# Where the second matrix of an MLP begins, and where weight sums, a late normalization and the last output product stand

## The chip, the cores and the metric

The kernel runs on one core of a Trainium2 chip. The metric is the device time of one execution in microseconds. Five engines work side by side, each on its own instruction list in order: TensorE (PE; its weight loads are PEld), VectorE (DVE), ScalarE (ACT), GpSimd (POOL) and SyncE (SP), which here issues nearly all DMAs. They wait for one another through semaphores.

## The reference

A transformer block on 2048 rows of 512: modulated layernorm, an attention in four segments of 512 rows with 32 heads of 16 and a memory M, z carried from segment to segment, an output projection, a second modulated layernorm, and an MLP of 1792 with gelu.

```python
h = _layernorm(x) * (1 + ca) + sa
for s in range(4):                       # inside _A_ref
    p = softmax(qs @ ks.T * scale + mask)
    a_mem = (phi(qs) @ M) / (phi(qs) @ z + 1e-6)
    o = g * a_mem + (1 - g) * (p @ vs)
    M, z = M + phi(ks).T @ vs, z + phi(ks).sum
x = x + ga * (o @ wo)
h = _layernorm(x) * (1 + cb) + sb
x = x + gb * (gelu(h @ w1 + b1) @ w2 + b2)
```

All matrices are fp32; the kernel splits most operands into a high and a low part (fp32r) and forms each product of 128 x 128 by 128 x 512 as three matmuls: high-high, low-high and high-low.

## The kernel before

The order of every engine's list is written out by hand (`manual_schedule`): instructions enter their engine's list in the order in which the Python code calls them.

First come the projections of the four segments (to about 190 us). Then the attention runs over 64 pairs of heads P; a "stack" Q is two pairs, a unit U is two stacks, four units make a segment. In each P the `order` strings of PRM place score parts for the row maxima of pair P + 4 (S), the exponentials of pair P (T), and slots c0 to c9. Work of other kinds has a position, ten times P plus the slot: `pv` (probabilities times values), `m_rows` and `m_put` (negative maxima, put into qst by a small DMA on ACT's queue), `load_stacks`, `pv_out` (stores TD), `pv_in`, `am_in`, `den`, `rb_in`, `mem_mix`, `mix`, `o_hi`, `o_lo` (the late normalization of a unit: the row sums dn go to memory as RD and come back spread out as rbB; memory term amB times rm; then the sum, and its split oh, ol). `ln` holds the positions at which the rows of segments 0 and 1 are loaded (`ln2_load`, tile xt), get statistics, `ln2_rstd` (crs, on POOL) and `ln2_apply`; `ht` those of the transposes `ln2_turn` of segment 0. `load_w1` fetches weight tiles wa for units 0 and 1 of the MLP at P = 58 and 60.

What is left over when the loop ends is called by `rest(U, names)` in the junction (L1102 to L1154): output products `wo_seg(s, b, gs)` of segments 2 and 3 (g counts the four units of a segment, b the four row blocks), their results `wo_out`, the transposes of segment 1, and the preparation of the MLP.

The MLP works in two passes p, each over two segments. Its first matrix w1 is multiplied by a scheme with seven products in place of eight for each pair of f blocks (a "quad" n; 7 quads a pass): b11, b21, t2, t1, t3, t4, b22 (`prod`). Their right sides are differences of the transposed rows (`r_sub`, split by `r_hi`, `r_lo`), their left sides the weights wa and the sums wb (`w_sub`, on POOL; split by `w_hi`, `w_lo`). X (bx), Y (by) and V (bv) are banks, two of each. t4 adds onto t3 in X, once ACT has copied t3 out (s3); b22 adds onto t2 in V. In `quad(n)` the two last products t4 and b22 of unit n - 1 stand between the products of unit n; an eighth call per pass does these alone (`last`). `g_out` does the gelu and stores a block to GD. `bg(n, i, ...)` hangs background work on step i of quad n.

The second matrix (`ffn2`) takes 28 steps m a pass, one g block each: twelve matmuls into four banks (`accs`). `load_g` brings g back from GD into a ring of four tiles, `split_g` splits it on ACT and DVE into a ring of three pairs. In pass 0 the w2 blocks are loaded in pairs (`load_w2`), scaled, and split on the way.

The tag wm has four buffers that wa, wb and w2r share in turn; amB had one.

Of the kernel before, what the change touches and what calls it, by code (L numbers as in the profile page):

```python
# [55 lines left out]
 'ht': [465, 474, 481, 494],  # L56
 'ln': [[312, 339, 374, 408], [560, 597, 612, 624]],
# [31 lines left out]
 'w1at': [58, 60],  # L89
 'mpre': 'a',  # L90
# [12 lines left out]
def block_kernel(ctx: ExitStack, tc: tile.TileContext, x, wq, wk, wv, wo, betaq, betam,  # L103
# [482 lines left out]
    with ExitStack() as pb:  # L586
# [255 lines left out]
        wa = {}  # L842
        NP = 64
# [122 lines left out]
    with ExitStack() as pc:  # L966
# [33 lines left out]
        wb = {}  # L1000

        def w_sub(j, i):
            if i == 0:
                wb[j] = wmp.tile([128, 4, 2, 128], F32, tag="wm", bufs=4, name=f"wb{j}")
            a, b = wa[j], wb[j]
            x, y = ((a[:, 2], a[:, 3]), (b[:, 0], a[:, 0]), (a[:, 0], a[:, 2]), (a[:, 1], b[:, 1]))[i]
            pool.tensor_tensor(out=b[:, i], in0=x, in1=y, op=ALU.add if i == 0 else ALU.subtract)  # L1007

# [37 lines left out]
        TAIL = 100  # L1046
# [4 lines left out]
        def quad(n, first, last):  # L1051
            def step(i):
                for f, a in bgs.pop((TAIL + n if last else n, i), ()):
                    f(*a)

            X, Y, V_, t2 = bx[n % 2], by[n % 2], bv[n % 2], s2[n % 2]
            X_, V__, t2_ = bx[(n - 1) % 2], bv[(n - 1) % 2], s2[(n - 1) % 2]
            if not last:
                prod(n, "b11", X, True)
                act.activation(s1, X, AF.Copy)  # L1060
            if not first:
                add(s3, V__)
                g_out(n - 1, s3, s3, 1, 1)
            step(0)
            if not last:
                prod(n, "b21", Y, True)
                add(s1, Y)
            step(1)
            if not first:
                prod(n - 1, "t4", X_, False)  # L1070
            if not last:
                g_out(n, s1, s1, 0, 0)
            if not first:
                g_out(n - 1, X_, s4, 1, 0)
            step(2)
            if not last:
                prod(n, "t2", X, False)
                act.activation(t2, X, AF.Copy)
            step(3)
            if not first:  # L1080
                prod(n - 1, "b22", V__, False)
                add(t2_, V__)
            step(4)
            if not last:
                prod(n, "t1", V_, True)
            if not first:
                g_out(n - 1, t2_, t2_, 0, 1)
            step(5)
            if not last:
                prod(n, "t3", X, False)  # L1090
                act.activation(s3, X, AF.Copy)
            step(6)
# [48 lines left out]
        r_hi(0, "t2")  # L1141
        for i in range(2, 4):
            w_lo(0, i)
# [96 lines left out]
        bg(6, 3, load_w2, 6)  # L1240
# [5 lines left out]
        ring = [[s1, s2[1 - p], s3, s4] for p in range(2)]  # L1246

        def load_g(p, m):
            sp.dma_start(ring[p][m % 4], GD[2 * p + m // FB][m % FB])

        def split_g(p, m):
            h, l = gx[0](f"gh{p}{m}"), gx[0](f"gl{p}{m}")
            ghs.append((h, l))
            split(h, l, ring[p][m % 4], v, act)
# [14 lines left out]

        for f in range(4, FB, 2):  # L1270
            if f + 4 < FB:
                fbg(0, f - 4, load_w2, f + 4)
            fbg(0, f - 4, scale_w2, f)
            fbg(0, f - 4, hi_w2, f)
            fbg(0, f - 3, lo_w2, f)
# [112 lines left out]
```

## Time and profile before

| | us |
|---|---|
| three timed runs | 819.32, 819.83, 821.99 (median 819.83) |
| the profiled execution | 820.48 |
| its span | 818.8 |
| PE busy | 788.6 |
| DVE, ACT, POOL busy | 555.7, 467.8, 333.9 |
| end of the projections, first scores | about 190 |
| last value product, first output product of segment 2 | 483.0 |
| first product of the MLP (b11 of quad 0) | 505.3 |
| first w2 product of pass 0, of pass 1 | 588.1, 736.5 |

A timeline row gives start, duration, engine, line, operation, output <- inputs with their shapes, how many were merged, and in brackets how long the engine stood idle before it and what released it. SPq and ACTq rows are the moments at which a DMA is issued, not its transfer. A window row gives for each engine the busy time in that stretch and the number of instructions, then the mean granted TensorE clock (1.00 is full), the share of the DMA engines in use and what they moved.

### The profile page before, as it was taken

Reading aid. Unit: us, or ns where it says so; the run is one execution under the profiler, and the core shown is the slowest. Engines: PE = TensorE matmul, PEld = TensorE weight load, DVE = VectorE, ACT = ScalarE, POOL = GpSimd, SP = SyncE. Lnnn points to the kernel's source line nnn. Section 1 sums busy time; section 2 is a strip of 40 time slices with the busy share of each in tenths; the row PEclk is TensorE's granted clock in tenths of the full one; section 3 lists DMA queues with packets and bytes.
Section 4 is the critical chain, followed back from the end, with each engine's and each line's share of the span. In section 5 each row is a group of like instructions: output and inputs, shape, how many; then the busy total and the mean of one; then the engine's idle time right before and its main releaser. Section 6 shows DMA issues by size and latency. Waiting matters only on the chain.

```text
span 818.8 us, 14152 instructions
## 1 busy us (share of the span) xinstructions
PE 788.6 (96%) x4585; PEld 535.2 (65%) x4585; DVE 555.7 (68%) x1405; ACT 467.8 (57%) x914; POOL 333.9 (41%) x558
## 2 busy tenths in 40 slices
PE   8999999999999999999999798999899999989998
PEld 4877777865444355445544246878688888868887
DVE  6685696569888877886688648875569765522423
ACT  3565645565787766776687574677553336652221
POOL 1347375542487645687766562342000313300000
PEclk9999999999999999999999899999999999999999
DMA  9597756594655675775667634755656624435443
GB/s 338 181 309 257 268 187 206 166 353 131 169 175 159 188 206 179 228 211 156 193 174 217 199 124 144 245 178 176 231 172 200 198 91 155 167 131 154 151 143 116
DMA packets 107522, 156.10 MB, mean 191 GB/s; under 512 B 16180, under 2 KB 55476, under 8 KB 107064
## 3 DMA queue, kind: packets, MB, share of 16 engines
q1 hardware_dynamic: 104952, 153.23, 58.4%
q10 hardware_dynamic: 2496, 1.97, 0.8%
q8 instruction: 36, 0.59, 0.3%
q14 instruction: 38, 0.31, 0.1%
HBM read 93.95 MB, written 60.83 MB: 189 GB/s over the span
## 4 chain that ended last, share of the span: by engine, by line
PE 75%; DVE 7%; ACT 6%; DMA 6%; issue 3%; POOL 3%; ACTq 0%; SPq 0%; DVEq 0%; POOLq 0%
PE bx L1032 8%; PE pv L737 7%; PE att L697 6%; PE att L608 6%; PE bx L1309 5%; PE q L314 5%; PE by L1309 5%; PE bv L1309 5%; PE bv L1032 4%; PE k L314 4%; PE v L465 3%; PE spare L1309 2%; PE mm L814 2%; PE mm L1309 2%; PE by L1032 2%
## 5 line engine op out<-in xcount | busy, mean ns | idle before, releaser
L615 DVE CUSTOM_DVE_ANT_0 dump<-att,maskb 128x512 bf16<-128x512 f32 (+2 forms) x384 | 192.4, 553 | 27.4 <-PE att L608 24.5
L712 ACT ACTIVATE pt<-att 128x512 f32<-128x512 f32 (+1 forms) x256 | 126.2, 560 | 45.3 <-PE att L697 44.9
L700 POOL TENSOR_SCALAR_AFFINE_SELECT pt<-pt 128x256 f32<-128x256 f32 x256 | 101.4, 413 | 82.8 <-ACT pt L712 49.0
L697 PE MATMUL att<-qst,kst 99*128 99x512 bf16 (+3 forms) x512 | 109.1, 304 | 7.2 <-ACT pt L723 3.0
L608 PE MATMUL att<-kst,qst 96*128 96x512 bf16 (+2 forms) x384 | 95.1, 330 | 2.8 <-DMA qst<-QD 2.4
L1007 POOL TENSOR_TENSOR wb<-wa 128x256 f32<-128x256 f32 x28 | 26.9, 962 | 155.5 <-DMA wa<-in_w 147.4
L737 PE MATMUL pv<-pt,V 128*32 128x512 f32 (+2 forms) x992 | 89.0, 450 | 0.0
L137 DVE TENSOR_TENSOR gl<-s,gh 128x512 fp32r<-128x512 f32 x56 | 39.9, 712 | 69.5 <-ACT gh L134 69.4
L697 PEld LDWEIGHTS <-kst 99*128 99x128 bf16 x512 | 43.5, 98 | 61.8 <-issue 43.0
L134 ACT ACTIVATE gh<-s 128x512 fp32r<-128x512 f32 x56 | 35.1, 630 | 83.2 <-PE spare L1309 38.9
L723 ACT ACTIVATE pt<-att 128x512 f32<-128x512 f32 (+1 forms) x128 | 56.9, 509 | 21.9 <-PE att L608 19.9
L608 PEld LDWEIGHTS <-qst 96*128 96x128 bf16 x384 | 33.4, 98 | 42.7 <-issue 25.2
L737 PEld LDWEIGHTS pv<-pt,V 128*32 128x32 f32 x992 | 22.3, 109 | 36.8 <-issue 27.1
L1041 DVE TENSOR_TENSOR s<-bv,s 128x512 f32<-128x512 f32 x28 | 19.3, 688 | 37.7 <-PE bv L1032 29.2
L619 DVE TENSOR_REDUCE nm<-att 128x2 f32<-128x256 f32 x64 | 27.2, 426 | 23.5 <-PE att L655 19.2
L1037 ACT ACTIVATE s<-s,b1t 128x512 f32<-128x512 f32 x42 | 30.3, 721 | 16.2 <-DVE s L1041 16.1
L615 DVE DVE_READ_ACCUMULATOR2_ANT nm<- 128x1 f32 x384 | 31.9, 83 | 0.0
L1309 PE MATMUL bx<-w2h,gh 128*128 128x512 f32 (+1 forms) x70 | 26.4, 377 | 4.1 <-ACT gh L134 4.1
L510 POOL TENSOR_TENSOR q<-qr,q 128x512 bf16<-128x512 f32 x16 | 18.7, 1167 | 27.9 <-ACT q L509 27.7
L501 POOL TENSOR_SCALAR qp<-qp 128x512 f32<-128x512 f32 x12 | 18.8, 1564 | 23.1 <-ACT qp L496 23.1
L1309 PE MATMUL bx<-w2h,gl 128*128 128x512 f32 (+1 forms) x70 | 26.4, 377 | 0.2 <-DVE gl L137 0.2
L314 PE MATMUL q<-Ahl,wqh 128*128 128x512 f32 x64 | 25.9, 404 | 0.5 <-DVE Ahl L137 0.5
(324 smaller groups left out, 2049.4 us busy)
## 6 DMA issues: line engine op xcount, KB each, us to landing
GD<-s SPq DMA_DIRECT2D x56, 256.0 KB
s<-GD SPq DMA_DIRECT2D x56, 256.0 KB
kst<-KD SPq DMA_DIRECT2D x32, 384.0 KB
qst<-QD SPq DMA_DIRECT2D x32, 384.0 KB
TD<-ts SPq DMA_DIRECT2D x32, 256.0 KB
wa<-in_w SPq DMA_DIRECT2D x28, 256.0 KB
QD<-q SPq DMA_DIRECT2D x16, 384.0 KB
KD<-k SPq DMA_DIRECT2D x16, 384.0 KB
```

The costliest lines, as they stand in the source:

```text
L134: act.activation(hi, src, AF.Copy)
L137: lo_eng.tensor_tensor(out=lo, in0=src, in1=hi.bitcast(F32), op=ALU.subtract)
L314: pe.matmul(ps, a[:, k, 128 * g:128 * g + 128], b[k], start=(k == 0 and i == 0), stop=(k == KB - 1 and i == 2))
L608: pe.matmul(ps, q_of(P, h, i), k_of(P, h, 128 * (i + 1)), start=True, stop=True)
L615: v.tensor_tensor_reduce(out=dump[n_dump[0] % 2][:, :n], in0=src, in1=maskb[:, 512 - n:], scale=-1.0, scalar=-4 * NEG, op0=ALU.add, op1=AL ...
L697: pe.matmul(ps, k[:99, e, 128 * j:128 * j + 128], q[:99, e, 128 * j:512], start=True, stop=True)
L700: pool.affine_select(out=t, in_=t, pattern=pattern, compare_op=ALU.is_ge, fill=0.0, base=0, channel_multiplier=-1)
L712: act.activation(pt[:, h, :], ps[:, :n], AF.Exp, scale=0.25)
L723: act.activation(pt, pv_, AF.Exp, scale=0.25)
L737: pe.matmul(ps[32 * c:32 * c + 32, lo:hi], V[4 * s + j][:, VW * hd:VW * hd + 32], pt[:, c % 2, lo - o:hi - o], start=start, stop=stop)
L1032: pe.matmul(ps, a[:, i, k, :], b[k], start=start and k == 0 and c == 0, stop=k == 1 and c == 2, skip_group_check=not start)
L1309: pe.matmul(ps, a[:, c], w[:, lo:hi], start=(f == 0 and i == 0), stop=(last and i == 2))
```

## The change

The positions of segment 0's transposes and of segment 1's layernorm are other ones; amB gets two buffers; `w_sub` is defined earlier, and for units 0 and 1 it runs on DVE at positions 642 and 650. In the junction the late normalization of unit 15, the splits and the third and fourth part (g = 2, 3) of segment 3's output products stand in other places; `close_wo` no longer has products and hangs on step 2 of quad 0. The eighth quad call is gone: after the seventh, the w2 steps begin, and t4 and b22 of the last unit follow steps 0 and 1 (`tail`). The first two g blocks of a pass get a tile of the tag wm (gr), loaded at step 1 of the last quad; the loads of w2 blocks 6 to 12 stand at steps 0, 1, 2 and 4 of the second matrix.

```diff
- 'ht': [465, 474, 481, 494],
- 'ln': [[312, 339, 374, 408], [560, 597, 612, 624]],
+ 'ht': [481, 501, 521, 541],
+ 'ln': [[312, 339, 374, 408], [590, 618, 630, 636]],
+ 'wsub': [642, 650],
-                am = so.tile([128, 512], F32, tag="amB", bufs=1, name=f"amB{U}")
+                am = so.tile([128, 512], F32, tag="amB", bufs=2, name=f"amB{U}")
+        def w_sub(j, i, e=pool):
...
+            e.tensor_tensor(out=b[:, i], in0=x, in1=y, op=ALU.add if i == 0 else ALU.subtract)
+        for j in range(2):
+            for i in range(4):
+                ap(PRM["wsub"][j] + i, w_sub, j, i, v)
+        def c22(n):
+            add(s3, bv[n % 2])
+            g_out(n, s3, s3, 1, 1)
+        def c21(n):
+            prod(n, "t4", bx[n % 2], False)
+        def c12(n):
+            prod(n, "b22", bv[n % 2], False)
+            add(s2[n % 2], bv[n % 2])
...
+        def tail(n, m):
+            if m == 0:
+                c21(n)
+                g_out(n, bx[n % 2], s4, 1, 0)
+            elif m == 1:
+                c12(n)
+                g_out(n, s2[n % 2], s2[n % 2], 0, 1)
-        rest(15, "pv_in")
-        for i in range(4):
-            w_sub(0, i)
+        rest(15, "pv_in", "am_in")
+        wo_seg(2, 0, range(4))
         r_hi(0, "b11")
         r_lo(0, "b11")
+        ln2_turn(1, 0)
         for i in range(2):
             w_hi(0, i)
         w_lo(0, 0)
-        wo_seg(2, 0, range(4))
-        ln2_turn(1, 0)
-        w_lo(0, 1)
-        r_hi(0, "b21")
-        r_lo(0, "b21")
+        rest(14, "mem_mix", "mix")
+        rest(15, "den", "rb_in")
         wo_seg(2, 1, range(4))
         ln2_turn(1, 1)
-        rest(14, "mem_mix", "mix", "o_hi")
-        rest(15, "den", "rb_in")
-        rest(15, "am_in")
+        rest(14, "o_hi")
+        w_lo(0, 1)
         wo_out(2, 0)
+        r_hi(0, "b21")
         rest(14, "o_lo")
+        r_lo(0, "b21")
         wo_seg(2, 2, range(4))
         ln2_turn(1, 2)
+        rest(15, "mem_mix")
         r_sub(0, "t1")
...
         for b in range(4):
             wo_seg(3, b, range(2))
+        rest(15, "mix", "o_hi")
         r_hi(0, "t1")
         r_hi(0, "b22")
-        rest(15, "mem_mix")
         wo_out(2, 2)
         wo_x(3, 1)
+        rest(15, "o_lo")
         r_lo(0, "b22")
+        for i in range(2, 4):
+            w_hi(0, i)
         r_sub(0, "t3")
         r_sub(0, "t2")
-        for i in range(2, 4):
-            w_hi(0, i)
-        r_hi(0, "t2")
-        for i in range(2, 4):
-            w_lo(0, i)
         wo_out(2, 3)
         wo_x(3, 2)
         wo_x(3, 3)
-        for i in range(4):
-            w_sub(1, i)
+        r_hi(0, "t2")
+        r_hi(0, "t3")
+        r_lo(0, "t2")
+        r_lo(0, "t1")
         for b in range(4):
-            wo_part(3, b, 2)
-        r_lo(0, "t2")
-        rest(15, "mix", "o_hi")
-        r_lo(0, "t1")
-        rest(15, "o_lo")
+            wo_seg(3, b, range(2, 4))
+        for i in range(2, 4):
+            w_lo(0, i)
+        r_lo(0, "t3")
         def close_wo():
-            for b in range(4):
-                wo_part(3, b, 3)
-        bg(0, 1, r_hi, 0, "t3")
-        bg(0, 2, r_lo, 0, "t3")
-        bg(0, 3, close_wo)
+        bg(0, 2, close_wo)
-        bg(6, 3, load_w2, 6)
         def load_g(p, m):
-            sp.dma_start(ring[p][m % 4], GD[2 * p + m // FB][m % FB])
+            if m == 0:
+                r = wmp.tile([128, 2, 512], F32, tag="wm", bufs=4, name=f"gr{p}")
+                graw[p, 0], graw[p, 1] = r[:, 0], r[:, 1]
+            elif m > 1:
+                graw[p, m] = ring[p][(m - 2) % 4]
+            sp.dma_start(graw[p, m], GD[2 * p + m // FB][m % FB])
         for p in range(2):
-            n = FH * p + FH
-            bg(n - 1, 5, load_g, p, 0)
-            bg(TAIL + n, 5, load_g, p, 1)
-            bg(TAIL + n, 5, load_g, p, 2)
-            bg(TAIL + n, 5, load_g, p, 3)
-            bg(TAIL + n, 6, split_g, p, 0)
-            bg(TAIL + n, 6, split_g, p, 1)
+            n = FH * p + FH - 1
+            bg(n, 1, load_g, p, 0)
+            bg(n, 1, load_g, p, 1)
+            bg(n, 5, load_g, p, 2)
+            bg(n, 5, split_g, p, 0)
+            bg(n, 6, split_g, p, 1)
+        for f, i in ((6, 0), (8, 1), (10, 2), (12, 4)):
+            fbg(0, i, load_w2, f)
         for p in range(2):
-            for j in range(FH + 1):
-                quad(FH * p + j, j == 0, j == FH)
+            for j in range(FH):
+                quad(FH * p + j, j == 0)
+            n = FH * p + FH - 1
+            c22(n)
+            load_g(p, 3)
             for m in range(NM):
...
                     ffn2(s, f, ghs.pop(0))
+                tail(n, m)
```

More of the change, by code (lines that the diff above doesn't have):

```diff
@@ L842, in block_kernel @@
         wa = {}
+        wb = {}
+        def w_sub(j, i, e=pool):
+            if i == 0:
+                wb[j] = wmp.tile([128, 4, 2, 128], F32, tag="wm", bufs=4, name=f"wb{j}")
+            a, b = wa[j], wb[j]
+            x, y = ((a[:, 2], a[:, 3]), (b[:, 0], a[:, 0]), (a[:, 0], a[:, 2]), (a[:, 1], b[:, 1]))[i]
+            e.tensor_tensor(out=b[:, i], in0=x, in1=y, op=ALU.add if i == 0 else ALU.subtract)
         NP = 64
@@ L1045, in block_kernel, with step @@
         bgs = {}
-        TAIL = 100
         def bg(n, i, f, *a):
             bgs.setdefault((n + i // 7, i % 7), []).append((f, a))
[L1051 to L1054, printed above, removed]
+        def step(n, i):
+            for f, a in bgs.pop((n, i), ()):
+                f(*a)
+        def c22(n):
[3 more added lines that the diff above has]
+            prod(n, "t4", bx[n % 2], False)
@@ L1056, in quad @@
+        def c12(n):
+            prod(n, "b22", bv[n % 2], False)
+            add(s2[n % 2], bv[n % 2])
+        def quad(n, first):
             X, Y, V_, t2 = bx[n % 2], by[n % 2], bv[n % 2], s2[n % 2]
[L1057 to L1060, printed above, removed]
+            prod(n, "b11", X, True)
+            act.activation(s1, X, AF.Copy)
             if not first:
-                add(s3, V__)
-                g_out(n - 1, s3, s3, 1, 1)
@@ L1064, in quad @@
[L1064 to L1068, printed above, removed]
+                c22(n - 1)
+            step(n, 0)
+            prod(n, "b21", Y, True)
+            add(s1, Y)
+            step(n, 1)
             if not first:
-                prod(n - 1, "t4", X_, False)
-            if not last:
-                g_out(n, s1, s1, 0, 0)
+                c21(n - 1)
+            g_out(n, s1, s1, 0, 0)
             if not first:
-                g_out(n - 1, X_, s4, 1, 0)
@@ L1075, in quad @@
[L1075 to L1079, printed above, removed]
-            if not first:
[L1081 to L1085, printed above, removed]
-            if not first:
[L1087 to L1091, printed above, removed]
@@ L1092, in quad @@
-            step(6)
+                g_out(n - 1, bx[(n - 1) % 2], s4, 1, 0)
+            step(n, 2)
+            prod(n, "t2", X, False)
+            act.activation(t2, X, AF.Copy)
+            step(n, 3)
+            if not first:
+                c12(n - 1)
+            step(n, 4)
+            prod(n, "t1", V_, True)
+            if not first:
+                g_out(n - 1, s2[(n - 1) % 2], s2[(n - 1) % 2], 0, 1)
+            step(n, 5)
+            prod(n, "t3", X, False)
+            act.activation(s3, X, AF.Copy)
@@ L1094, in wo_seg @@
+            step(n, 6)
+        def tail(n, m):
[5 more added lines that the diff above has]
+                g_out(n, s2[n % 2], s2[n % 2], 0, 1)
         def wo_seg(s, b, gs):
@@ L1253, in split_g @@
             ghs.append((h, l))
-            split(h, l, ring[p][m % 4], v, act)
+            split(h, l, graw.pop((p, m)), v, act)
         for p in range(2):
-            n = FH * p + FH
-            bg(n - 1, 5, load_g, p, 0)
-            bg(TAIL + n, 5, load_g, p, 1)
-            bg(TAIL + n, 5, load_g, p, 2)
-            bg(TAIL + n, 5, load_g, p, 3)
-            bg(TAIL + n, 6, split_g, p, 0)
-            bg(TAIL + n, 6, split_g, p, 1)
+            n = FH * p + FH - 1
[4 more added lines that the diff above has]
+            bg(n, 6, split_g, p, 1)
         fs = {}
```

10 lines of the change are left out of this document (1 added, 9 removed).

## The prediction

> **What bounds the kernel now.** I read the page first (totals and the clock line), then the timeline of PE alone for its idle times, then windows around them. The profiled execution took 820.48 us, 0.65 above the median of the three runs shown; its span is 818.8.
>
> ```profile
> span 818.8 us, 14152 instructions
> PE 788.6 (96%) x4585; PEld 535.2 (65%) x4585; DVE 555.7 (68%) x1405; ACT 467.8 (57%) x914; POOL 333.9 (41%) x558
> ```
>
> PE is busy nearly throughout, so removable time is where PE waits or runs slowly. These are its waits behind 440 us that the edits can reach:
>
> ```profile
> 453.52 1.04 PE L608 MATMUL att<-kst,qst 96*128 96x512 bf16 x2 [2.36 <-DMA qst<-QD]
> 469.00 0.23 PE L676 MATMUL mm<-identb,nm 128*128 128x128 bf16 x1 [1.60 <-POOL nm L671]
> 490.15 0.66 PE L576 MATMUL mm<-ident,xt 128*128 128x128 f32 x4 [0.89 <-ACT hr L578]
> 511.14 0.78 PE L1032 MATMUL bx<-rt2h,w1mh 128*128 128x512 f32 x1 [3.00 <-ACT s L1060]
> 583.04 0.50 PE L1032 MATMUL bx<-rt4h,w1th 128*128 128x512 f32 x1 [0.74 <-ACT s L1091]
> 588.13 0.51 PE L1309 MATMUL bx<-w2h,gh 128*128 128x512 f32 x1 [2.06 <-ACT gh L134]
> 731.38 0.50 PE L1032 MATMUL bx<-rt4h,w1th 128*128 128x512 f32 x1 [0.74 <-ACT s L1091]
> 736.46 0.79 PE L1309 MATMUL bx<-w2h,gh 128*128 128x512 f32 x1 [2.06 <-ACT gh L134]
> ```
>
> They add up to 13.5 us, but each costs more than itself. Windows (columns: PE, PEld, DVE, ACT, POOL busy, clock, DMA share, GB/s) show a half clock after each group:
>
> ```profile
> 453.10:460.00 6.90, 6.48 (x25) 2.18 (x26) 3.02 (x10) 2.19 (x5) 0.41 (x1) 0.51 0.48 149
> 470.20:473.60 3.40, 3.40 (x29) 0.92 (x18) 0.00 (x0) 2.77 (x7) 3.15 (x7) 0.50 0.22 61
> 511.20:514.60 3.40, 3.40 (x8) 2.73 (x9) 2.95 (x5) 3.37 (x6) 0.00 (x0) 0.50 0.95 311
> 589.65:593.05 3.40, 3.40 (x10) 2.62 (x9) 1.56 (x3) 1.26 (x2) 0.00 (x0) 0.51 1.02 351
> 736.40:739.80 3.40, 3.34 (x7) 2.42 (x8) 0.69 (x1) 0.63 (x2) 0.00 (x0) 0.51 0.87 281
> ```
>
> At half clock a stretch of 3.4 us does 1.7 us of work. The four parts below are these four places.
>
> **The two tails (terms C and D).** Before, each pass ends with t4 and b22 of its last unit alone on PE: t4 waits until ACT has copied t3 out of the same bank, and the first w2 product waits for b22, its add, its gelu, and the split of g block 0 behind that gelu on ACT. The change starts w2's steps 0 and 1 right after t3, t4 behind step 0 and b22 behind step 1. No PE instruction is added; 12 products move per pass, with the adds, gelus and stores behind them.
>
> ```profile
> 672.16 2.72 PE bx L1032 x12
> 581.92 0.39 PE L1032 MATMUL bx<-rt3l,w1mh 128*128 128x512 f32 x1
> 593.30 0.40 PE L1309 MATMUL bx<-w2h,gl 128*128 128x512 f32 x1
> 730.25 0.39 PE L1032 MATMUL bx<-rt3l,w1mh 128*128 128x512 f32 x1
> 741.29 0.39 PE L1309 MATMUL bx<-w2h,gl 128*128 128x512 f32 x1
> 582.39 0.60 ACT L1091 ACTIVATE s<-bx 128x512 f32<-128x512 f32 x1 [1.31 <-PE bx L1032]
> 590.82 1.31 ACT L134 ACTIVATE gh<-s 128x512 fp32r<-128x512 f32 x2 [2.75 <-DMA s<-GD]
> 580.23 1.29 DVE L1227 TENSOR_TENSOR w2l<-w2r,w2h 128x512 fp32r<-128x512 f32 x2
> ```
>
> Twelve matmuls in a row take 2.72, 0.227 each. From t3's last matmul to the second of step 1 there are 26 such steps (12 of t4 and b22, 12 of step 0, two more): 5.90 us unhindered. The first tail took 593.30 - 581.92 = 11.38, the second 741.29 - 730.25 = 11.04; the losses are 5.48 and 5.14, waits and half clock together. Afterwards ACT's 0.60 copy lies under step 0 (2.72), and b22 has all of step 1. The new cost: step 0's g must be split before t3 ends. Its load now goes to buffers of its own (gr), issued a quad earlier; on DVE its low half stands behind the w2l pair that ends at 581.5, so it is done near 582.4 when PE wants it at 582.4. If that cover fails in the first tail, the load wait of 2.75 appears, perhaps with 1.7 of half clock: lower bound 5.48 - 4.45 = 1.0. The second tail has no w2 load in its queue; there a short wait might still bring the half clock, 5.14 - 1.7 = 3.4. Nearest is the row of DVE, which is on time, so I take off 0.35 each: C = 5.1 and D = 4.8. On SP the gr loads stand ahead of two stores of the last quad, the load of w2 block 6 goes from the last quad to step 0, and the load of g block 5 now waits for the store of t4's result; behind it stand the w2 loads (R4).
>
> **The junction (term B).** Here the change finishes the weight sums wb on DVE under the end of attention, runs the late normalization of unit 15 before segment 3's products, and brings those products' third and fourth part ahead of b11. Before, the fourth part (g=3) sat behind t2. On SP the loads of amB and rm go ahead of unit 15's RD store, which waits for DVE.
>
> ```profile
> 483.03 0.50 PE L814 MATMUL bx<-woh,oh 128*128 128x512 f32 x1
> 518.31 0.39 PE L1032 MATMUL bx<-rt3h,w1mh 128*128 128x512 f32 x1
> 484.30:522.80 38.50, 34.62 (x152) 27.93 (x151) 33.36 (x48) 19.15 (x34) 14.24 (x14) 0.96 0.52 172
> 504.36 0.96 DVE L1022 TENSOR_TENSOR w1tl<-wa,w1th 128x256 fp32r<-128x256 f32 x1
> 520.82 0.41 DVE L1022 TENSOR_TENSOR w1tl<-wa,w1th 128x256 fp32r<-128x256 f32 x1
> ACT oh L128 <- DVE opk L788: 6.4, 2, 4.9
> ```
>
> The last row is from the waits: ACT stood 4.9 us before oh of unit 15, and the copy of b11 that releases t2 (the 3.00) stood behind it. PE needed 35.28 us from the first output product to t3 for 120 matmuls (27.2) and four groups of transposes (0.66 each, 2.6): 5.5 lost. All 120 stand in this stretch afterwards too, so 5.5 is the upper bound. DVE sets what is reached: it is busy 33.36 of 38.50 here, and has the same list to do up to rt4l. The same operation takes 0.41 alone and 0.96 beside POOL's sums; eight sums leave POOL here, so eight times 0.55 = 4.4 us come off DVE. I take B = 4.4, lower bound 2.0, if half of it goes into new waits of DVE for ACT and PE. Where the stall goes: DVE is next, at rt4l before t4 of unit 0.
>
> The sums cost DVE eight times 0.41 to 0.96, 3.3 to 7.7, after the last score row; the window 470.20 shows it empty there (0.00 of 3.40), so on the path they cost 0 to 1, inside B.
>
> The Trainium skill ("SBUF — State Buffer", section "Who interferes with whom") says that a VectorE operation with two SBUF inputs and a GpSimd operation that reads SBUF lock each other out completely. The 0.41 and 0.96 agree. By that rule the moved sums would hold up POOL's masks, eight times 0.41 = 3.3 us, and the time would be 804.5 instead of the sum below.
>
> **The end of attention (term A).** The 1 MB load of segment 1 (xt) moves from behind the last stack load to behind wa, rm and xb; its statistics, rstd and normalization, and the transposes of segment 0, move later; amB gets a second buffer.
>
> ```profile
> 435.55 0.31 SPq L748 DMA_DIRECT2D TD<-ts  x1
> 443.50 0.33 SPq L748 DMA_DIRECT2D TD<-ts  x1
> 444.35 0.47 SPq L176 DMA_DIRECT2D qst<-QD  x1
> 444.88 0.49 SPq L558 DMA_DIRECT2D xt<-X2D  x1
> 455.99 0.59 SPq L781 DMA_DIRECT2D rbB<-RD  x1
> 456.69 0.40 SPq L748 DMA_DIRECT2D TD<-ts  x1
> 465.95 0.33 SPq L748 DMA_DIRECT2D TD<-ts  x1
> 448.00:452.00 4.00, 3.16 (x38) 1.44 (x30) 3.04 (x13) 3.79 (x9) 2.25 (x6) 1.00 1.03 280
> 471.82 0.23 POOL L149 TENSOR_SCALAR crs<-cmv 128x4 f32<-128x4 f32 x1
> 472.13 1.05 POOL L150 TENSOR_TENSOR crs<-crs,neg_half 128x4 f32<-128x4 f32 x1
> 476.04 0.78 DVE L786 TENSOR_TENSOR opk<-opk,rbB 128x512 f32<-128x512 f32 x1 [6.71 <-DMA rbB<-RD]
> ```
>
> A TD store marks each stack: 7.95 between the first two, 13.19 over the stall, 9.26 in the half clock: 5.24 + 1.31 = 6.55 above the pace. In between the DMA engines are full (1.03, 280 GB/s). The stack's last load, issued at 444.35, let PE go at 453.5; without 1 MB (3.6 us at 280 GB/s) sharing the engines it lands near 450, before PE is ready at 453.52 - 2.36 = 451.2. SP also stood until 455.99 for the small RD store behind xt, with TD behind it. New on POOL: crs (0.23 + 1.05) now stands before the last four masks, 1.3 to 1.5 us, waiting for statistics that stand behind a mix on DVE (the one that waited 6.71 for rbB); behind crs wait those masks, and for them the last value products of PE. A = 6.55 - 1.5 = 5.0. Upper bound 8.1, if the 1.60 wait for nm goes too and crs costs nothing; lower -1.5, crs alone. The transposes only move, with their ACT copies, between products of the same kind: 0. The second amB buffer lets SP pass a wait of under 1 us: in the bounds.
>
> **The sum.** 5.0 + 4.4 + 5.1 + 4.8 = 19.3; 820.48 - 19.3 = 801.2. Bounds: gains of 4.9 (-1.5 + 2.0 + 1.0 + 3.4) to 24.2 (8.1 + 5.5 + 5.5 + 5.1), so 815.6 to 796.3.
>
> **Rivals.** R1: the stack load is late because of what stands before it, not xt behind it: A = 0, 820.48 - 14.3 = 806.2. For it: the engines were already full before, and xt was issued 0.5 us later. Against: RD stood in the same queue until 455.99. The Trainium skill ("DMA: Bandwidth & Descriptors", section "Queues, rings and completion order") says that each engine consumes a ring in order; by that alone xt behind qst delays nothing, which is R1's time.
>
> R2: DVE becomes the bound of the junction: the sums (up to 7.7) run into the splits of b11 and the mix of unit 15 comes no earlier; B = 0, 805.6. For: 33.36 of 38.50 busy. Against: the empty window.
>
> R3: the early g loads land late in the first tail, under full DMA queues; minus 2.75 and 1.7, 805.6. Against: the data was stored five quads earlier and more, and the buffer is free by then.
>
> R4, slower: w2 blocks 6, 8, 10 and 12 are now loaded inside the second matrix, on SP behind g loads that wait for a store of this very tail (s4). If each pair came late by its two steps (5.44), four pairs cost 21.8 against 19.3: 823.0. It decides once a pair lands over 4.8 us after its step. For: SP is in order, and one such wait was 2.75. Against: block 6 is first used at step 6, 6 x 2.72 + 2 x 1.36 = 19 us after t3.
>
> R5: the waits only change their names, and the end is within 0.3% of 820.
>
> **How the numbers follow.** Forecast 0.55 (its own range 797 to 804), R1 0.18, R2 0.12, R3 0.08, R4 0.05, R5 0.02. A measurement here tells 0.3% (2.5 us) from no change. The first four are faster: 0.93; same 0.02; slower 0.05. The range 796.5 to 809 takes in the forecast and R1 to R3; left out are R4, R5 and the pairs of R1 to R3.
>
> **What would show it.** Right: no PE wait over 0.5 us between t3 and step 3 of either pass, no half clock there; TD stores at 8 us up to the last; oh of unit 15 not waited for 4 us; PE's next wait at t4 of unit 0. Wrong: a PE wait for qst at the same stack (R1), rb11l late behind the sums on DVE (R2), gh waiting for gr (R3), PE waiting for w2h at step 6 (R4).

## The result, and the profile after

The changed kernel took 810.92 us (median of four runs, 809.77 to 814.46), the kernel before, timed beside it, 820.91 (819.32 to 824.56): a ratio of 0.988, 95% interval 0.983 to 0.993. The gain is 10 us, about half of the 19.3 forecast, and the time lies above the predicted range. The profiled execution took 810.60, its span is 808.9. One of the executions reported below, 818.43 us in a5_sums_before_mix, was a slow one: it counts in the median given there (808.77 without it) but not in the ratio.

The page's totals after; busy times, shares and counts:

```profile
span 808.9 us, 14151 instructions
PE 782.7 (97%) x4585; PEld 531.5 (66%) x4585; DVE 555.5 (69%) x1413; ACT 467.2 (58%) x914; POOL 327.0 (40%) x550
```

PE has the same 4585 matmuls. From before to after the span falls by 9.9 and PE's busy time by 5.9; the rest was waiting. To see where, five rows cut the timeline into stretches: the TD store near 425 (stack 24, counted from 0), the first output product, the last t3 of pass 0, the first b11 of pass 1, the last t3 of pass 1. After:

```profile
425.11 0.34 SPq L749 DMA_DIRECT2D TD<-ts  x1
483.03 0.50 PE L815 MATMUL bx<-woh,oh 128*128 128x512 f32 x1
578.82 0.39 PE L1036 MATMUL bx<-rt3l,w1mh 128*128 128x512 f32 x1
661.29 0.39 PE L1036 MATMUL bx<-rb11h,w1mh 128*128 128x512 f32 x1
724.98 0.39 PE L1036 MATMUL bx<-rt3l,w1mh 128*128 128x512 f32 x1
```

and the rows of before that the prediction does not already show:

```profile
427.18 0.34 SPq L748 DMA_DIRECT2D TD<-ts  x1
666.56 0.39 PE L1032 MATMUL bx<-rb11h,w1mh 128*128 128x512 f32 x1
```

| stretch | before | after | gain | predicted |
|---|---|---|---|---|
| 1: TD store of stack 24 to first output product (A) | 55.85 | 57.92 | -2.1 | 5.0 |
| 2: to the last t3 of pass 0 (B) | 98.89 | 95.79 | 3.1 | 4.4 |
| 3: to the first b11 of pass 1 (C) | 84.64 | 82.47 | 2.2 | 5.1 |
| quads of pass 1 | 63.69 | 63.69 | 0.0 | 0 |
| 4: last t3 of pass 1 to the last matmul (D) | 84.91 | 79.96 | 4.95 | 4.8 |

To this comes a start that is 2.1 earlier already (427.18 to 425.11). D is as predicted, B and C fall short, and the end of the attention has become longer, not shorter. A second profile of each kernel (below) gives the same picture: stretch 1 56.18 before and 59.96 after, stretch 2 98.74 and 95.79, stretch 3 84.99 and 82.83.

PE's waits over 0.42 us behind 458, after:

```profile
458.09 1.41 PE L698 MATMUL att<-qst,kst 99*128 99x128 bf16 x5 [0.62 <-ACT pt L713]
462.47 0.23 PE L677 MATMUL mm<-identb,nm 128*128 128x128 bf16 x1 [1.59 <-POOL nm L672]
468.84 1.19 PE L698 MATMUL att<-qst,kst 99*128 99x512 bf16 x3 [2.94 <-DMA qst<-ms]
479.06 4.04 PE L738 MATMUL att<-pt,V 128*32 128x512 f32 x28 [2.42 <-POOL pt L701]
517.95 0.50 PE L1036 MATMUL bx<-rt4h,w1th 128*128 128x512 f32 x1 [1.33 <-ACT s L1096]
519.14 0.50 PE L1036 MATMUL bx<-rt4l,w1th 128*128 128x512 f32 x1 [0.45 <-DVE rt4l L1010]
608.28 0.49 PE L1320 MATMUL bx<-w2h,gh 128*128 128x512 f32 x1 [0.64 <-ACT gh L135]
```

The wait for qst at 453.5, the 3.00 in the junction and both waits of each tail are gone. Two waits at the end of the attention have come instead: the one for ms (2.94) is new, and the one for the last masks has grown to 2.42. In the first profile of before it was 0.75, with no half clock behind it, but in the second it was 2.06, with one:

```profile
480.76 2.35 PE L737 MATMUL att<-pt,V 128*32 128x512 f32 x28 [0.75 <-POOL pt L700]
479.89 3.68 PE L737 MATMUL att<-pt,V 128*32 128x512 f32 x28 [2.06 <-POOL pt L700]
```

Each of the two waits after has a half clock behind it, 0.50 from 469.5 to 472 and from 480 to 482; these windows run past its end (columns as in the prediction's windows):

```profile
470.20:473.60 3.40, 3.40 (x22) 0.87 (x18) 0.59 (x1) 1.89 (x6) 1.00 (x3) 0.67 0.49 154
480.40:483.80 3.40, 3.40 (x25) 1.65 (x18) 3.33 (x8) 0.60 (x2) 1.27 (x1) 0.66 0.09 21
```

What leads to them, in the timeline and one window after:

```profile
457.86 0.42 SPq L559 DMA_DIRECT2D xt<-X2D  x1
459.79 1.88 SPq L839 DMA_DIRECT2D wa<-in_w  x2
462.09 1.62 SPq L776 DMA_DIRECT2D RD<-dn  x1
463.04 0.73 ACTq L680 DMA_DIRECT2D qst<-ms  x1
468.96 0.60 SPq L782 DMA_DIRECT2D rbB<-RD  x1
460.00:464.00 4.00, 2.41 (x31) 0.93 (x23) 0.00 (x0) 2.31 (x7) 3.65 (x8) 1.00 1.06 292
473.01 0.86 DVE L787 TENSOR_TENSOR opk<-opk,rbB 128x512 f32<-128x512 f32 x1 [4.48 <-DMA rbB<-RD]
475.42 0.66 DVE L564 BATCH_NORM_STATS2 cst<-xt 128x6 f32<-128x512 f32 x1
476.38 0.57 POOL L150 TENSOR_SCALAR crs<-cmv 128x4 f32<-128x4 f32 x1 [1.44 <-DVE cmv L565]
```

The 1 MB load (xt) and w1 (wa, 0.5 MB) fill the DMA engines (share 1.06). The 12 KB of maxima of stack 31 (ms), issued at 463.04, let PE go on at 468.84, and SP stands until 468.96 for the small store RD. Then rbB lands, DVE mixes, and only then come the last statistics, crs and, behind crs, POOL's last masks.

### The profile page after: what moved, and what is told of

The parts are those of the page before. It is cut to its first block, busy times and chain, and to the rows that moved or that the text cites. A ratio compares the mean times of both kernels' runs of the same rounds, so it can differ in the third digit from the quotient of the medians.

```text
span 808.9 us, 14151 instructions
## 1 busy us (share of the span) xinstructions
PE 782.7 (97%) x4585; PEld 531.5 (66%) x4585; DVE 555.5 (69%) x1413; ACT 467.2 (58%) x914; POOL 327.0 (40%) x550
## 4 chain that ended last, share of the span: by engine, by line
PE 73%; DVE 7%; DMA 7%; ACT 5%; issue 3%; POOL 3%; SPq 1%; ACTq 0%; DVEq 0%; POOLq 0%
PE bx L1036 8%; PE pv L738 7%; PE att L698 6%; PE att L609 5%; PE q L315 5%; PE bx L1320 4%; PE k L315 4%; PE bv L1036 4%; PE by L1320 4%; PE bv L1320 4%; PE v L466 3%; PE mm L815 2%; PE spare L1320 2%; PE by L1036 2%; DMA RD<-dn 1%
## 5 line engine op out<-in xcount | busy, mean ns | idle before, releaser
L851 POOL TENSOR_TENSOR wb<-wa 128x256 f32<-128x256 f32 x24 | 22.8, 950 | 162.6 <-DMA wa<-in_w 162.6
L138 DVE TENSOR_TENSOR gl<-s,gh 128x512 fp32r<-128x512 f32 x52 | 36.7, 706 | 66.9 <-ACT gh L135 66.9
L135 ACT ACTIVATE gh<-s 128x512 fp32r<-128x512 f32 x52 | 32.4, 629 | 74.8 <-PE spare L1320 31.7
L315 PE MATMUL q<-Ahh,wqh 128*128 128x512 f32 x64 | 25.9, 405 | 0.2 <-DVE Ahh L137 0.2
```

What stands on the lines that cost most here:

```text
L135: act.activation(hi, src, AF.Copy)
L138: lo_eng.tensor_tensor(out=lo, in0=src, in1=hi.bitcast(F32), op=ALU.subtract)
L315: pe.matmul(ps, a[:, k, 128 * g:128 * g + 128], b[k], start=(k == 0 and i == 0), stop=(k == KB - 1 and i == 2))
```

## The experiments

All are the changed kernel with one part moved, except where said. Stretches 1 to 3 as above; each stretch is of one profiled execution. What the expectations call the TD store of stack 25 and of stack 26 are the rows at 425.11 and 433.02, those of stacks 24 and 25. Counted from 0 in the same way, the maxima that wait behind the load at 560 are those of stack 29; the expectation of before_again calls them stack 30.

| run | stretch 1 | 2 | 3 | median us | ratio to before, 95% |
|---|---|---|---|---|---|
| before_again | 56.18 | 98.74 | 84.99 | 820.63 | 0.997 to 1.001 |
| after_again | 59.96 | 95.79 | 82.83 | 812.23 | 0.986 to 0.992 |
| a1_old_load | 56.06 | 95.31 | 81.47 | 812.61 | 0.985 to 0.994 |
| a2_early_load | 58.20 | 96.28 | 82.82 | 812.06 | 0.984 to 0.994 |
| a3_stats_before_mix | 54.34 | 96.19 | 82.11 | 809.74 | 0.981 to 0.989 |
| a4_early_load_late_stats | 60.55 | 96.22 | 82.24 | 813.51 | 0.983 to 0.995 |
| a5_sums_before_mix | 54.10 | 96.22 | 83.06 | 809.62 | 0.980 to 0.986 |
| a6_load_583_sums_before_mix | 55.24 | 96.27 | 82.98 | 809.83 | 0.981 to 0.990 |
| b1_sums_on_pool | 57.49 | 95.47 | 82.42 | 811.89 | 0.985 to 0.990 |
| b2_old_junction_order | 57.97 | 95.36 | 82.30 | 811.95 | 0.984 to 0.991 |
| c1_splits_later | 57.07 | 95.09 | 79.29 | 807.09 | 0.978 to 0.984 |
| best_load_behind_ms_and_splits_later | 54.13 | 99.92 | 80.38 | 806.88 | 0.980 to 0.986 |
| a_and_c_repaired | 53.88 | 96.83 | 80.20 | 807.21 | 0.981 to 0.987 |
| a_c_and_old_junction | 54.74 | 94.83 | 79.27 | 804.35 | 0.979 to 0.985 |

Executions of one kernel differ by several us, so the stretches say more than the medians. They vary as well: where no edit aims at it, stretch 2 lies between 95.09 and 96.83 (99.92 with the load at 612) and stretch 3 between 81.47 and 83.06, and with the changed kernel's end of the attention (after, after_again, b2, c1) stretch 1 lies between 57.07 and 59.96.

**The end of the attention (A).**

```diff
- 'ln': [[312, 339, 374, 408], [590, 618, 630, 636]],
+ 'ln': [[312, 339, 374, 408], [560, 597, 612, 624]],   # a1_old_load
+ 'ln': [[312, 339, 374, 408], [550, 580, 615, 624]],   # a2_early_load
+ 'ln': [[312, 339, 374, 408], [590, 612, 622, 636]],   # a3_stats_before_mix
+ 'ln': [[312, 339, 374, 408], [550, 618, 630, 636]],   # a4_early_load_late_stats
```

> The changed kernel with the old places of segment 1's load, statistics, rstd and normalization (560, 597, 612, 624); the new places of segment 0's transposes and the second amB buffer stay. Theory T1 (the 1 MB load delays the small transfers behind it wherever it stands): the wait for qst of about 2.4 us and the half clock near 451 come back, the waits for ms of stack 31 (2.94) and for the last masks (2.42) go; the first output product stays at 482 to 484.5, the time at 811 (809.5 to 812.5). Theory T3 (the load is harmless, only the statistics and crs behind the mix of unit 13 cost): first output product at 479, time 807. Theory T2 (the end of the attention is bound by something else than the load and crs): 483 and 811, but without the qst wait.

> The changed kernel with segment 1's load, statistics, rstd and normalization at 550, 580, 615 and 624: the load stands ahead of the last stack load by a P and the statistics and crs stand ahead of the mix of unit 13. T1: the qst wait, the wait for ms of stack 31 and the wait for the last masks all go, with their half clock; first output product at 476.5 to 478, time 804.5 to 806. T3: 479 and 807. T2: 483 and 811. If the load is in the way at its new place too (ms of stack 28 or 29, RD of unit 12): 480 to 483 and 808 to 811.

> The changed kernel with the load at its place (590), but statistics at 612 to 621 and rstd at 622, ahead of the mix of unit 13 (623). T1: the wait of the last masks for crs (2.42) and the half clock behind it go, the wait for ms of stack 31 (2.94) with its half clock stays; first output product at 479 to 481, time 807 to 809. T3: 479 and 807. T2: 483 and 811.

> The changed kernel with the load alone moved to 550; statistics, rstd and normalization stay at 618, 630 and 636, behind the mix of unit 13. T1: with the load out of the way the wait for ms of stack 31 goes, rbB of unit 13 comes some 4 to 5 us earlier, and with it the mix, the statistics and crs; first output product within 1 us of the kernel with everything early (476.5 to 478.5), time 804.5 to 807. T3: crs still stands behind a late mix: 480 to 481, time 808 to 809. T2: 483 and 811.

Putting the load back (a1) brought a small transfer's wait back at 453, here 1.62 for ms of stack 29, and took the one at 468 away; the wait for the last masks stayed, so T1 was right on the load and wrong on the masks. Earlier still (a2, a4) the load stands ahead of the last stack load, and PE waits for that: 3.31 and 3.75. The early load was no way out: the first output product came 5.8 and 10 behind the latest times that T1 gave (478 and 478.5), and PE waited 2.39 and 3.75 for the last masks as well.

```profile
453.42 1.03 PE L609 MATMUL att<-kst,qst 96*128 96x512 bf16 x2 [3.31 <-DMA qst<-QD]
```

Statistics ahead of the mix (a3) did what T1 said: ms of stack 31 still waited 2.74, the last masks 0.67, and the first output product is at 481.12, at the end of T1's range. Stretch 1 is 3.6 shorter than in the first profile of the changed kernel, and 2.7 to 5.6 shorter than in the four profiles with its end of the attention.

In a1 crs is early too, and still the last masks were late. Its rows, of POOL, PE and DVE:

```profile
475.63 3.15 POOL L701 TENSOR_SCALAR_AFFINE_SELECT pt<-pt 128x256 f32<-128x256 f32 x4 [1.23 <-ACT pt L713]
477.85 4.04 PE L738 MATMUL att<-pt,V 128*32 128x512 f32 x28 [2.26 <-POOL pt L701]
475.98 0.68 DVE L804 TENSOR_TENSOR ol<-opk,oh 128x512 fp32r<-128x512 f32 x1
476.58 0.41 DVE L851 TENSOR_TENSOR wb<-wa 128x256 f32<-128x256 f32 x1
477.02 0.51 DVE L851 TENSOR_TENSOR wb<-wb,wa 128x256 f32<-128x256 f32 x1
```

Four masks took 3.15 from the first to the last while DVE ran the split of ol and the moved sums; in a5 below they take 2.24 (474.00 to 476.24). The next two runs move the sums into DVE's idle time before the mix; a6 puts the load at a third place as well.

```diff
- 'wsub': [642, 650],
+ 'wsub': [614, 618],
- 'ln': [[312, 339, 374, 408], [590, 618, 630, 636]],
+ 'ln': [[312, 339, 374, 408], [560, 597, 612, 624]],   # a5_sums_before_mix
+ 'ln': [[312, 339, 374, 408], [583, 600, 612, 636]],   # a6_load_583_sums_before_mix
```

> As a1_old_load (segment 1 in its old places), but the weight sums of units 0 and 1 stand on DVE at 614 to 621, ahead of the mix of unit 13, while DVE waits for rbB, and no longer at 642 to 653 beside the last masks of POOL. Theory M (the sums and POOL's last masks lock each other out: four masks took 3.15 us in a1_old_load, 1.5 would be their pace; PE's wait of 2.26 and the half clock of the last value products, 4.04 instead of 2.35 us, follow from that): four masks in 1.5 to 2.3, PE's wait for them 0.8 or less, the last 28 value products in 2.35, so the first output product 2.5 to 3.3 us earlier against the stack before it, near 478.6 to 479.5; time 1.5 to 3.3 below a1_old_load. Rival (crs or the exponentials on ACT make the last masks late): wait of 2.2 and half clock stay, first output product 481.8, same time as a1_old_load.

> The 1 MB load at 583 (behind the stack loads and the TD store of stack 27, ahead of the loads of unit 13), statistics from 600, rstd at 612, normalization at 636, the sums at 614 to 621. T1 and M together: the qst wait, the ms waits over 1 us, and the wait of the last masks all go, with their half clock; first output product at 475.5 to 478, 43 to 45 us after the TD store of stack 26 where the changed kernel took 50.0 (433.02 to 483.03); time 804 to 806.5. If the load now delays ms of stack 30 or RD of unit 13 as it did ms of stack 31: one wait of 1.5 to 3 with half clock is left, 479 to 481, time 807 to 809. If neither the load nor the sums matter: 483 and 811.

The rows of a5 that answer to those of a1:

```profile
474.00 0.93 POOL L701 TENSOR_SCALAR_AFFINE_SELECT pt<-pt 128x256 f32<-128x256 f32 x2 [1.03 <-ACT pt L713]
475.47 0.77 POOL L701 TENSOR_SCALAR_AFFINE_SELECT pt<-pt 128x256 f32<-128x256 f32 x2 [0.54 <-ACT pt L724]
474.00 3.32 PE L738 MATMUL att<-pt,V 128*32 128x512 f32 x32
```

PE does not wait for the masks here, and the clock stays full: from the TD store of stack 30 to the first output product it is 2.33 where a1 took 5.26. In this pair theory M holds, and the last two runs below, with the sums at the same early place, agree: PE waits 0.40 and 0.79 for the last masks, and 28 value products take 2.35. Stretch 1 as a whole is only 1.96 shorter, in part because ms of stack 29 waited longer (2.16 to 1.62).

The sums are not the only thing that makes the last masks late. In a3 they stood where the changed kernel has them, and PE waited 0.67; in b1 below they were on POOL again, with crs still behind the mix, and PE waited 2.74, where M had expected less; in before_again no sum ran on DVE, and PE waited 2.06. A second path leads from a late mix to the masks: the last exponentials stand behind oh of unit 13 in ACT's list, and oh waits for the mix. Rows of before_again (oh, then the four masks) and of after_again (oh):

```profile
476.82 0.63 ACT L128 ACTIVATE oh<-opk 128x512 fp32r<-128x512 f32 x1 [1.19 <-DVE opk L788]
478.28 2.28 POOL L700 TENSOR_SCALAR_AFFINE_SELECT pt<-pt 128x256 f32<-128x256 f32 x4 [2.04 <-ACT pt L712]
477.83 0.63 ACT L129 ACTIVATE oh<-opk 128x512 fp32r<-128x512 f32 x1 [3.44 <-DVE opk L789]
```

No run moves oh alone, so what this path costs is open. In a6 the wait for the last masks is gone too, but ms of stacks 30 and 31 waited 1.18 and 1.78: the load met its next neighbours. That is the middle case of its expectation, which it missed by 0.9 (first output product at 481.86).

**The junction (B).**

```diff
-        for j in range(2):
-            for i in range(4):
-                ap(PRM["wsub"][j] + i, w_sub, j, i, v)
...
         rest(15, "pv_in", "am_in")
+        for i in range(4):
+            w_sub(0, i)
...
         wo_x(3, 3)
+        for i in range(4):
+            w_sub(1, i)
```

> The changed kernel with the weight sums of units 0 and 1 back on POOL in the junction (unit 0 at its begin, unit 1 behind the loads of xb); all else as changed. Term B as predicted (POOL's sums slow DVE, 0.96 against 0.41, eight times 0.55 = 4.4): from the first output product to the first matmul of t4 39.4 instead of 34.9, to the last t3 of pass 0 3 to 4.4 longer than 95.8. Rival (the gain came from the new places of the late normalization and of segment 3's products, the sums are hidden): 34.9 to 36 and 95.8 to 96.8. At the end of the attention M expects the wait for the last masks to fall (crs may keep 1 of the 2.42), the first output product up to 3 earlier; so the time 810 to 812 by B and M, 807 to 809 by the rival and M.

That was the edit of b1. b2 puts the junction's lines of the kernel before (from `rest(15, "pv_in")` to `close_wo` with its fourth part of the products) in place of the changed ones, without the `w_sub` calls.

> The changed kernel with the junction's old order (late normalization of unit 15, splits, third and fourth part of segment 3's output products where they stood before); the weight sums stay on DVE under the end of the attention, the tails as changed. If the sums had been the brake of the junction, as term B said, most of the gain stays: first output product to the first matmul of t4 35 to 36.5. If it is the order (b1_sums_on_pool kept the whole gain with the sums on POOL): 38.5 to 39.5, the wait of t2 for ACT's copy of b11 (3.00 before) and its half clock come back, and to the last t3 98 to 99 instead of 95.8; time 2.5 to 3.5 above the changed kernel, 813.5 to 814.5.

The row of b1 to compare; its first output product is at 485.13, so t4 comes 34.26 later (34.92 in the changed kernel, 39.36 before):

```profile
519.39 0.50 PE L1033 MATMUL bx<-rt4h,w1th 128*128 128x512 f32 x1 [0.59 <-ACT s L1093]
```

With the sums back on POOL nothing of the gain is lost, so they did not have to leave it. But b2, with the sums away and the old order, keeps the gain as well: t4 comes 35.56 behind the first output product, as its first case expected. In stretch 2: with neither 98.89 and 98.74 (before), sums alone 95.36, order alone 95.47, both 95.79. Either is enough, and together they bring no more.

Two things limit this. "Neither" is the kernel before, which lacks the other parts of the change too; no run has those parts with the sums on POOL and the old order. And b1 does not bring the contention back in full. Windows from the first output product to t4, of before, b1 and b2 (DVE is the third column):

```profile
483.03:522.39 39.36, 35.48 (x156) 28.61 (x155) 32.95 (x47) 20.11 (x35) 14.71 (x14) 0.96 0.52 171
485.13:519.39 34.26, 33.67 (x156) 27.40 (x154) 30.01 (x47) 19.85 (x34) 9.69 (x9) 1.00 0.50 158
481.44:517.00 35.56, 34.09 (x156) 27.52 (x154) 30.26 (x50) 19.92 (x35) 5.46 (x5) 0.99 0.57 184
```

DVE needs 2.9 less in b1 for the same 47 instructions, and 3.9 less in b2 if its three sums of 0.42 are left out. So both edits relieve DVE, which is what term B was about.

**The second matrix (C).** The edit moves nothing but the calls of r_hi, r_lo and r_sub for pass 1.

```diff
-        for f, fn, n in ((4, r_hi, "b11"), (5, r_lo, "b11"), (6, r_hi, "b21"), (7, r_lo, "b21"), (8, r_sub, "t1"),
-                         (9, r_hi, "b22"), (9, r_hi, "t1")):
-            fbg(0, f, fn, 1, n)
...
+        for s, f, fn, n in ((0, 10, r_hi, "b11"), (0, 11, r_lo, "b11"), (0, 12, r_hi, "b21"), (0, 13, r_lo, "b21"),
+                            (1, 0, r_sub, "t1"), (1, 1, r_hi, "b22"), (1, 1, r_hi, "t1"), (1, 2, r_lo, "b22"),
...
+            fbg(s, f, fn, 1, n)
```

> The changed kernel with the splits and differences of pass 1's right sides (r_hi, r_lo, r_sub) moved from steps 4 to 23 of pass 0's second matrix to steps 10 to 25, behind the preparation of w2. Theory S (the chain of splits between ACT and DVE, 7.16 us per two steps with these splits in it against PE's 5.44, eats the lead of g and w2): PE's small waits between 600 and 616 (2.75 together) go, from the last t3 to b11 of pass 1 79.2 to 80 instead of 82.5, time 2 to 3 less, 808 to 809. Rival L (the loads of w2 and g come late behind the stores of the tail, which costs before step 8): 82 to 82.5 and 811. In between (80 to 82): both.

Splits of w2 on ACT, in the changed kernel and in c1:

```profile
598.27 1.24 ACT L1230 ACTIVATE w2h<-w2r 128x512 fp32r<-128x512 f32 x2 [1.36 <-DVE w2r L1226]
605.44 1.23 ACT L1230 ACTIVATE w2h<-w2r 128x512 fp32r<-128x512 f32 x2 [3.85 <-DVE w2r L1226]
612.60 1.23 ACT L1230 ACTIVATE w2h<-w2r 128x512 fp32r<-128x512 f32 x2 [3.85 <-DVE w2r L1226]
```

```profile
595.11 1.24 ACT L1230 ACTIVATE w2h<-w2r 128x512 fp32r<-128x512 f32 x2 [1.36 <-DVE w2r L1226]
600.03 1.23 ACT L1230 ACTIVATE w2h<-w2r 128x512 fp32r<-128x512 f32 x2 [2.64 <-DVE w2r L1226]
604.95 1.24 ACT L1230 ACTIVATE w2h<-w2r 128x512 fp32r<-128x512 f32 x2 [2.64 <-DVE w2r L1226]
```

A pair of w2 blocks came every 7.16 us, PE uses one in 5.44; without the splits of pass 1 it comes every 4.92. PE's waits between 600 and 616 are gone and stretch 3 is 3.2 shorter, all of theory S. The late loads of theory L cost nothing that shows here: in c1 too the fourth and fifth pair come 7.50 and 6.68 behind the one before, and PE does not wait.

**Together.** Load at 612, behind everything small, with the late splits:

```diff
- 'ln': [[312, 339, 374, 408], [590, 618, 630, 636]],
+ 'ln': [[312, 339, 374, 408], [612, 626, 637, 640]],
- 'wsub': [642, 650],
+ 'wsub': [614, 618],
```

> The 1 MB load of segment 1 at 612, behind the last ms transfer, RD and rbB of unit 13; statistics from 626 (behind the mix of unit 13), rstd at 637 and normalization from 640, behind the last masks; the sums at 614 to 621; the splits of pass 1 later as in c1_splits_later. From the TD store of stack 25 to the first output product the changed kernel took 57.9, the kernel before 55.9, a5_sums_before_mix 54.1. T1 and M: no small transfer is left behind the load and no mask beside the sums, so 51.5 to 53.5, no wait for ms of stack 30 or 31 over 1 us; from the last t3 to b11 of pass 1 79.3; time 802 to 804.5. If w1 and the loads of units crowd the queue without the 1 MB as well: 54 to 56, time 804.5 to 806.5. If the normalization now comes too late for the transposes of segment 1: a new wait of PE of 1 to 3 us behind the first output products.

Nothing waits for ms, but PE waited 1.58 for a stack load (449.65) with no 1 MB near it. Stretch 1, 54.13, is in the second case of the expectation, not the first. The late statistics and normalization now lie in the junction, and stretch 2 is 99.92, 4.1 longer: PE waits 1.02 and 2.62 for ACT there, and ACT up to 5.10 for DVE's mix. What the end of the attention won was lost behind it.

> The changed kernel once more, for a second profile: the same waits (ms of stack 31 near 2.3 to 2.9, the last masks near 2 to 2.7), from the TD store of stack 25 to the first output product 57 to 58.5, time 809 to 813.

> The kernel before once more, for a second profile of the end of its attention: if the stall behind the 1 MB load is its own, qst or ms of stack 30 waited 1.6 to 2.5 with half clock again, the last masks waited under 1; TD store of stack 25 to the first output product 55 to 57.

In after_again ms of stack 31 waited only 0.98 and the last masks 5.38, so how the loss divides between the two changes from run to run; stretch 1, 59.96, is longer than expected. In before_again it was ms of stack 29 that waited (2.10), and the last masks 2.06, more than expected. Last, a5 and c1 in one kernel, with the changed and with the old junction:

> a5_sums_before_mix and c1_splits_later together. If the two losses are separate: TD store of stack 25 to the first output product 53.5 to 55 (changed kernel 57.9 and 60.0), first output product to last t3 95.5 to 96.5, last t3 to b11 of pass 1 79.2 to 79.6 (82.5), so 6 to 8 below the changed kernel: 803.5 to 805.5. If the early end of the attention only makes another wait longer: one of the three stretches takes 2 or more back, and the time stays at 806.5 to 808, as in c1_splits_later alone.

> As a_and_c_repaired, with the junction's old order. As in b2_old_junction_order the sums alone should be enough: first output product to last t3 95 to 96, time within 1 of a_and_c_repaired. If the new order is needed when unit 15's normalization is not held up at the end: 97.5 to 99, time 2 to 3 more than a_and_c_repaired.

The page of the second:

```profile
span 802.6 us, 14146 instructions
PE 781.1 (97%) x4585; PEld 532.3 (66%) x4585; DVE 556.5 (69%) x1413; ACT 466.9 (58%) x914; POOL 325.0 (40%) x550
```

With the changed junction 1.7 came back in stretch 2 and 0.9 in stretch 3 against c1 (96.83 and 80.20, against 95.09 and 79.29), and the median is that of c1 alone: the second case of its expectation. With the old junction the three stretches are 54.74, 94.83 and 79.27, and the median is 804.35 (803.19 to 808.96), 6.6 below the changed kernel and inside the predicted range. It was expected within 1 of the other and came 2.9 below it. It is the lowest median of all, but its ratio to the kernel before (0.979 to 0.985) is no better than c1's (0.978 to 0.984), so that it is faster than c1 is not shown.

## Why the prediction was wrong

**A, predicted 5.0, measured -2.1: the step that failed.** The prediction priced what the 1 MB load cost at its old place and gave it no price at the new one. That the stall behind it would go was right; "TD stores at 8 us up to the last" was wrong. The last four stores after:

```profile
459.42 0.33 SPq L749 DMA_DIRECT2D TD<-ts  x1
469.67 0.39 SPq L749 DMA_DIRECT2D TD<-ts  x1
477.10 0.32 SPq L749 DMA_DIRECT2D TD<-ts  x1
483.82 0.32 SPq L749 DMA_DIRECT2D TD<-ts  x1
```

They are 10.25, 7.43 and 6.72 apart, where before they are 8.13, 6.02 and 3.73. Wherever the load stood between 550 and 590, the next small transfers waited: the stack load at 550, ms of stack 29 or the stack load at 560, ms of stacks 30 and 31 at 583, ms of stack 31 at 590. Where neither crs nor the sums hold up the last masks, the load at 560 gives 53.9 to 54.7 (a5 and the last two runs) and at 590 54.3 (a3): moving it is worth nothing. The best of these, 53.88, is 2.0 below before; 5.0 was never reached. This is rival R1's A = 0, not for its reason, since the transfers that waited stand behind the load or beside it.

The second fault was the place of crs behind the mix. It was seen, priced at 1.5 and as a lower bound, without what feeds it: RD and rbB were held up by the same load, and a half clock follows. a3 puts it at 3.6, or at 2.7 to 5.6 by all four profiles. The third was "on the path they cost 0 to 1" for the sums: DVE's empty window (470.20 to 473.60) lies ahead of the mix (476.04), while the sums at 642 and 650 stand behind the mix in DVE's list, where they can meet the last masks. From a1 to a5 they cost 1.96 in stretch 1, 2.93 behind stack 30, by one pair of profiles; in a3 they did no harm that shows.

The Trainium skill ("SBUF — State Buffer", section "Who interferes with whom") says that a VectorE instruction with two SBUF inputs contends with a GpSimd instruction that reads SBUF. The masks of a1 and a5 agree with it in kind: four took 3.15 beside the sums and 2.24 without them. The prediction weighed this rule at 3.3 and left it out of the sum; the sum should have held a price for it, though by a1 and a5 a smaller one.

**B, predicted 4.4, measured 4.44 at the named place and 3.1 at the end: a right size, the reason in part open.** The first matmul of t4 comes 4.44 earlier, and it is there that PE waits next, for ACT and for rt4l, as said. That DVE was the brake agrees with b1 and b2, which both relieve it by 3 to 4 and bring t4 forward by 5.1 and 3.8. That the sums had to leave POOL for it is refuted by b1. The prediction summed one cause where the change made two moves of which each was enough, so that the size agreed is in part luck. What sets the 95 that all variants but one reach was not isolated; the two small waits at t4 and what follows took back 1.3.

**C, predicted 5.1, measured 2.2.** The tail went as forecast: step 0 starts at 579.04, 0.22 behind the last t3, with no half clock, and R3's late g did not come. The error was to end the working at step 1. The splits of w2 and of pass 1's right sides need 7.16 per pair of steps, before as after. But before, the two pairs ahead of them came 4.9 apart, and after, 7.51 and 6.24: the pair of blocks 10 and 11 is split 22.4 behind the first w2 product before and 26.4 after, so the lead on PE is gone. Whether the tail's adds and gelus, which now stand among these splits, or the later loads took it was not isolated. R4 looked at this place, but at the loads. With that chain relieved (c1) the stretch is 79.29, a gain of 5.35 from before.

**D, predicted 4.8, measured 4.95: right.** Pass 1 has no w2 to prepare, and is the control for C.

**The sum.** -2.07 + 3.10 + 2.17 + 4.95 is 8.15; with the 2.1 by which stack 24 was stored earlier it is 10.2, the distance of the last matmuls. The earlier start is not explained: 14 profiles with changes have this store between 422.7 and 427.9, the two of before at 427.2 and 427.3. Of the 11.2 that are missing from the 19.3, A has 7.1 and C 2.9.

## What to carry to other kernels

A big load that is moved off one small transfer lands on the next one: list what is issued in the 10 us behind its new place, and what waits for each, before a gain is written down. When a stall goes, work the preparation chain behind it through to its end, with its period against that of the engine it feeds, since it may live on a lead that the change uses up. And a gain that agrees in size does not prove its reason: undo the supposed cause alone, and look whether the cost that it is said to have comes back with it.

## What was unexpected of the hardware

A transfer of 12 KB on ACT's queue took 5.8 us from its issue to PE's release (463.04 to 468.84) beside 1.5 MB on SP's, at a DMA share of 1.06 from 460 to 464 and 0.77 from 463 to 469.

The half clock came after waits shorter than its own 3.4 us, and not after each. The last 28 value products took 4.04 after a wait of 2.26 (a1, above; the window from 478.00 below is its own), and 2.35 after one of 1.79 in c1 (the second row):

```profile
478.00:481.40 3.40, 3.40 (x28) 1.45 (x21) 3.37 (x7) 0.00 (x0) 2.06 (x3) 0.54 0.36 119
```

```profile
478.00 2.35 PE L738 MATMUL att<-pt,V 128*32 128x512 f32 x28 [1.79 <-POOL pt L701]
```

The Trainium skill ("TensorE: Matmul & The Clock Gate", section "HAM oscillation — how this bites in real kernels") gives as its rule no idle gaps over about 3.4 us; here 2.26 was enough. The length of a wait alone does not decide: one of 1.60 before (469.00) was followed by 0.50 from 470.20 to 473.60, and one of 2.62 in the run with the load at 612 (518.15) by 1.00 in the 3.4 us behind it.
